# First batch of a pooled-attention and feed-forward kernel: V product and key transposes ahead of the scores, a second query buffer, weights touched two steps later

## The chip, the core and the metric

The kernel runs on one core of a Trainium2 chip. A core has five engines with a queue each: TensorE (PE in the profile; its weight loads are PEld), VectorE (DVE), ScalarE (ACT), GpSimd (POOL) and SyncE (SP, which here issues nearly all transfers). The metric is device time in microseconds, the median of the runs; lower is better.

## What is computed

Four batches of attention with 8 heads, 1152 keys and a head size of 64. The queries are averaged in pairs, so there are 576 of them. The output of all heads of a batch is the input of a feed-forward block with layer norm and a residual.

```python
q_pool = q.reshape(B, H, S // 2, 2, D).mean(axis=3)         # B, H, S, D = 4, 8, 1152, 64
scores = scale * np.matmul(q_pool, k.transpose(0, 1, 3, 2))
attn = softmax(scores)                                       # max, exp, sum, divide
x = np.matmul(attn, v)            # heads side by side: (4, 576, 512)
xn = (x - mean) / sqrt(var + 1e-6) * g_ln
out = x + np.maximum(xn @ w_ch1, 0.0) @ w_ch2                # 512 -> 2048 -> 512
```

All tensors are float32. Most products are done as three float16 products of high and low halves (`hi`, `lo`).

## The kernel before

**Steps.** The 32 heads form 16 pairs, a pair has C = 9 score tiles of 128 queries by 1152 keys, so there are 144 steps, numbered i, with p = i // 9 the pair. `step(i)` issues the work of one step to all engines in an order written out by hand; each engine then takes its own instructions strictly in that order and waits where data is missing. The first batch is pairs 0 to 3, steps 0 to 35; `on_pe(i)` is true there.

**One step of the first batch.** The scores S(i+1) go to three PSUM banks, 0 to 2 or 3 to 5 by turns (`slot`). DVE takes the row maximum (`emit_max`, L337) and makes the bias nb (L338), ACT takes the exponential into `pe` (`emit_exp`, L343), PE transposes `pe` in nine pieces back into the banks of the scores (`emit_t`, L376, called T(i) here), and ACT copies the result out to `pt` in two halves (`emit_t_copy`, L382). Because S(i+2) uses the same banks as S(i), it waits for these copies. The V product of an earlier tile (`emit_pv`, L400, PV here) is float32, and its result is scaled by 1/sum in `evac_pv` (DVE L446 and L449, ACT L453). In the later batches ACT and DVE make the halves `hl` instead, and a DMA transposes them (L369).

**What else is in the first batch.** The keys and queries of the next pair are transposed on PE, one piece a step (`prep_k`, `prep_q`, lines 275 to 289), and split into halves by ACT (L264) and DVE (L265). The 16 MB of float32 weights come in 32 pieces m of 512 KB, piece m issued in step m on SP (`w_load`, L633). ACT reads a piece first (`w_bias`, L638), then DVE passes over it three times (`w_conv`, L106), PE forms column sums of it (`w_sums`, L665), and after eight pieces a bound is reduced (`w_reduce`, and `all_max` at L194 to L203). POOL then splits four pairs of pieces into halves (`w_splits`, L238 and L721). Steps 36 to 143 add the feed-forward products as units (L534, L565).

**Order.** Lists say in which step a thing is issued: `pre(i, ...)` at the start of step i, `at(i, ...)` at its end. `fill` holds the DVE passes over weights, dripped one by one between other work; `evacs` holds what `flush` issues in the next step; `reds` the parts of a bound. The query tile `qr` holds two pairs and has one buffer; the bank pair 6 and 7 (`bank()`) takes the transposes of keys and queries.

The functions that the change touches follow with the line numbers of the profile.

Of the kernel before, what the change touches and what calls it, by code (L numbers as in the profile page):

```python
# [24 lines left out]
def tile_pooled_attention_moe(  # L25
# [158 lines left out]
    def all_max(src, n, then):  # L184
# [4 lines left out]
        def place():  # L189
            return psum[:, 3 * (pv_slot[0] % 2) + 2, 258:386]  # L190
# [18 lines left out]
    reds = deque()  # L209
# [51 lines left out]
    def split_from(ps, s, hi, lo):  # L261

        return (
            lambda: nc.scalar.activation(out=hi, in_=ps, func=ACTF.Copy, scale=s),  # L264
            lambda: nc.vector.scalar_tensor_tensor(lo, ps, s, hi, op0=ALU.mult, op1=ALU.subtract),  # L265
        )

    def prep_k(p, u):
# [3 lines left out]
        if u < 2:  # L272
# [3 lines left out]
            return split_from(ps, s[:, 0:1], kt[:, 0, u, 0:512], kt[:, 1, u, 0:512])  # L276
# [3 lines left out]
        return split_from(x, s[0:64, 0:1], kt[0:64, 0, :, 512:640], kt[0:64, 1, :, 512:640])  # L280

    def prep_q(p, u):
# [10 lines left out]
        return split_from(ps[:, 0:384], s[:, 1:2], qt[:, 0, c], qt[:, 1, c])  # L293
# [17 lines left out]
    def emit_s(i):  # L311
# [330 lines left out]
    def w_conv(m):  # L642
# [15 lines left out]
        later(lambda: sums.append(lambda: w_sums(part, 2 * c + z, lo)))  # L658
# [75 lines left out]

    for p in range(1, NP):
# [4 lines left out]
        if p % 2 == 0:  # L740
            at(i0 - 1, load_q, p, (nc.sync,))
# [115 lines left out]
    def some_units(i):  # L857
        if preps:
            fn, p, u = preps.popleft()
            evacs.extend(fn(p, u))  # L860
        for _ in range(1 if i < NSTEP + 5 else 2):
# [3 lines left out]
    def a_piece(i):  # L865
        pieces.extend(ready.pop(i, ()))
        for u in range(2 if len(pieces) > 2 else 1):
# [6 lines left out]
    def step(i):  # L874
# [15 lines left out]
        while sums and i % 2 == 0:  # L890
            sums.popleft()()
        flush()
        if live:
# [19 lines left out]
    with tc.manual_schedule():  # L913
# [52 lines left out]
        i = 0  # L966
# [32 lines left out]
```

## Time and profile before

| what | value |
|---|---|
| device time, median of 3 runs | 969.31 us (957.99, 969.43, 969.31) |
| span of the profiled execution | 963.9 us |
| PE busy | 880.9 us, 91% |
| DVE, ACT, POOL busy | 627.4, 549.9, 346.4 us |
| step 0's row maximum starts | 21.53 us |
| step 36's row maximum starts | 255.74 us |
| bytes moved | 114.92 MB |

For the profiled execution no device time is given beside its span; the span lies 5.4 us under the median and 5.9 us over the lowest run. Times in the profile count from the start of the span. A matmul's end is modelled, so neighbouring matmuls can overlap by some tenths. The busy shares are means over stages that differ: the first batch, steps 36 to about 130 in which attention and feed-forward overlap, and a tail with the feed-forward alone.

### The profile page before, as it was taken

The page shows a single profiled execution, that of the slowest core. Times are in us where ns is not written, and L with a number is a line of the kernel's source. Part 1 is how long each engine was busy: PE and PEld are TensorE (multiplying, and loading weights), DVE is VectorE, ACT ScalarE, POOL GpSimd, SP SyncE. Part 2 cuts the span into 40 slices and gives each one's busy share as a digit, 9 for nine tenths or more (in the row PEclk, how much of TensorE's full clock was granted, in tenths as well). Part 3 has the DMA queues.
Part 4 walks back from the last instruction along what each step waited for, and adds up shares of the span by engine and source line. Part 5 has one row for each costly group of instructions (what it writes and reads, how often), then busy time and mean ns, then how long its engine had stood idle before and what let it go on. Part 6 is the DMA issues. An engine that isn't in the chain of part 4 may idle for free.

```text
span 963.9 us, 21832 instructions
## 1 busy us (share of the span) xinstructions
PE 880.9 (91%) x9286; PEld 628.5 (65%) x9286; DVE 627.4 (65%) x1160; ACT 549.9 (57%) x779; POOL 346.4 (36%) x315
## 2 busy tenths in 40 slices
PE   5897988999869899989698999999989999999998
PEld 4676766777747476666474757566765766767665
DVE  4576696767787577757875777678777777542221
ACT  3765465655476677667667677676676766411000
POOL 3002165243579352435543424344534241310000
PEclk7897797968889999999999999999999999999999
DMA  5325152150155988698959596969596886600000
GB/s 156 145 70 183 66 177 69 48 183 1 50 99 106 191 125 171 129 197 133 179 102 209 102 198 129 187 131 174 101 208 118 168 143 116 122 23 12 12 12 22
DMA packets 271665, 114.92 MB, mean 119 GB/s; under 512 B 254928, under 2 KB 254928, under 8 KB 271568
## 3 DMA queue, kind: packets, MB, share of 16 engines
q1 hardware_dynamic: 271216, 112.65, 56.2%
q8 instruction: 72, 1.18, 0.5%
q10 hardware_dynamic: 352, 0.88, 0.3%
q14 instruction: 25, 0.20, 0.1%
HBM read 45.09 MB, written 4.72 MB: 52 GB/s over the span
## 4 chain that ended last, share of the span: by engine, by line
PE 57%; DVE 20%; ACT 9%; DMA 7%; issue 3%; SPq 3%; POOL 0%; ACTq 0%; DVEq 0%; POOLq 0%
PE psum L534 14%; PE psum L565 14%; PE psum L324 8%; PE psum L400 7%; PE psum L411 7%; DVE mx L337 5%; DMA pt<-hl 4%; DVE hl L366 4%; ACT pt L382 3%; PE psum L376 3%; DMA stage<-in_moe_w_ch_dram 2%; DVE ht L548 2%; PE psum L289 2%; SPq L128 2%; DVE kt L265 1%
## 5 line engine op out<-in xcount | busy, mean ns | idle before, releaser
L337 DVE TENSOR_REDUCE mx<-psum 128x1 f32<-128x1152 f32 x144 | 194.4, 1350 | 76.6 <-PE psum L400 39.6
L343 ACT ACTIVATE pe<-psum,nb,sc 128x1152 f32<-128x1152 f32 x144 | 188.9, 1312 | 29.5 <-DVE nb L338 28.2
L565 PE MATMUL psum<-wsl,ht 128*128 128x512 f16 x864 | 199.0, 383 | 0.2 <-DVE ht L548 0.2
L324 PE MATMUL psum<-kt,qt 64*128 64x512 f16 (+3 forms) x1440 | 166.3, 342 | 28.2 <-ACT pt L382 17.0
L534 PEld LDWEIGHTS <-wsl 128*128 128x128 f16 x1920 | 172.8, 99 | 25.1 <-issue 3.0
L534 PE MATMUL psum<-xn,wsl 128*128 128x256 f16 x1536 | 181.2, 277 | 2.1 <-DVE xn L504 1.1
L324 PEld LDWEIGHTS <-qt 64*128 64x128 f16 (+1 forms) x1440 | 70.6, 99 | 114.4 <-issue 76.0
L565 PEld LDWEIGHTS <-ht 128*128 128x128 f16 x864 | 82.5, 99 | 92.2 <-issue 4.3
L357 ACT ACTIVATE hl<-pe 128x1152 f16<-128x1152 f32 x108 | 125.7, 1164 | 19.5 <-DMA pt<-hl 16.2
L453 ACT ACTIVATE xb<-psum,r 128x64 f32<-128x64 f32 x128 | 40.1, 313 | 150.6 <-DVE r L449 142.1
L411 PEld LDWEIGHTS <-pt 128*128 128x128 f16 (+1 forms) x3240 | 108.9, 101 | 22.6 <-issue 22.1
L411 PE MATMUL psum<-vt,pt 128*128 128x65 f16 (+1 forms) x3240 | 120.5, 195 | 0.0
L366 DVE SCALAR_TENSOR_TENSOR hl<-pe,hl 128x1152 f16<-128x1152 f32 x72 | 104.9, 1457 | 0.0
L238 POOL TENSOR_SCALAR pe<-pe 128x1152 f32<-128x1152 f32 x36 | 42.0, 1166 | 153.9 <-ACT hl L357 143.6
L548 DVE SCALAR_TENSOR_TENSOR ht<-psum,ht 128x512 f16<-128x512 f32 x72 | 49.6, 690 | 72.6 <-ACT ht L547 71.8
L547 ACT ACTIVATE ht<-psum 128x512 f16<-128x512 f32 x72 | 42.8, 594 | 93.7 <-PE psum L534 93.3
L400 PE MATMUL psum<-vt,pt 128*128 128x65 f32 (+1 forms) x720 | 96.1, 298 | 0.0
L400 PEld LDWEIGHTS psum<-vt,pt 128*128 128x128 f32 (+1 forms) x720 | 91.9, 213 | 3.6 <-issue 3.4
L364 POOL TENSOR_TENSOR hl<-pe,hl 128x1152 f16<-128x1152 f32 x36 | 85.4, 2373 | 3.0
L382 ACT COPY pt<-psum 128x512 f32<-128x512 f32 x72 | 44.7, 639 | 55.9 <-PE psum L376 55.1
L161 POOL TENSOR_TENSOR qr<-qr 128x1152 f32<-128x1152 f32 (+1 forms) x8 | 22.3, 2786 | 130.2 <-DMA qr<-in_q_dram 94.6
L376 PE MATMUL psum<-ident,pe 128*128 128x128 f32 x324 | 51.7, 315 | 5.1 <-ACT pe L343 4.9
(104 smaller groups left out, 898.6 us busy)
## 6 DMA issues: line engine op xcount, KB each, us to landing
stage<-in_moe_w_ch_dram SPq DMA_DIRECT2D x32, 512.0 KB, 6.7
kr<-in_k_dram SPq DMA_DIRECT2D x16, 576.0 KB, 4.4
qr<-in_q_dram SPq DMA_DIRECT2D x31, 288.0 KB, 5.6
vr<-in_v_dram SPq DMA_DIRECT2D x15, 576.0 KB, 5.0
out_dram<-xb SPq DMA_DIRECT2D x32, 128.0 KB, 2.5
pt<-hl SPq DMA_TRANSPOSE x108, 4.8
vr<-in_v_dram ACTq DMA_DIRECT2D x1, 576.0 KB, 6.1
out_dram<-xh SPq DMA_DIRECT2D x4, 128.0 KB, 3.5
```

Of the source, the lines that this page charges most:

```text
L324: nc.tensor.matmul(out=sp[o:o + w, c0:c0 + n], lhsT=qt[r:r + 64, qa, q0:q0 + w], rhs=kt[r:r + 64, ka, h, k0:k0 + n], start=(a == 0), stop= ...
L337: nc.vector.tensor_reduce(mx, st["s"], axis=AX.X, op=ALU.max)
L343: nc.scalar.activation(out=st["pe"], in_=st["s"], func=ACTF.Exp, scale=pair[i // C]["sc"][:, 0:1], bias=st["nb"],)
L357: nc.scalar.activation(out=hl[:, 0], in_=st["pe"], func=ACTF.Copy, scale=2.0 ** 15)
L364: nc.gpsimd.tensor_tensor(hl[:, 1], st["pe"], hl[:, 0], op=ALU.subtract)
L366: nc.vector.scalar_tensor_tensor(hl[:, 1], st["pe"], 2.0 ** 15, hl[:, 0], op0=ALU.mult, op1=ALU.subtract)
L376: nc.tensor.transpose(st["s"][:, n], st["pe"][:, n], ident)
L382: nc.scalar.copy(st["pt"][:, a:b], st["s"][:, a:b])
L400: nc.tensor.matmul(out=dst, lhsT=pt[:, 128 * u + q0:128 * u + q0 + w], rhs=vt[:, h, c], start=(u == 0), stop=(u == C - 1),)
L411: nc.tensor.matmul(out=dst[:, 0:n], lhsT=lhsT, rhs=rhs, start=(u == 0 and lhsT is hi and n == 65), stop=(u == C - 1 and lhsT is lo), skip_ ...
L534: nc.tensor.matmul(out=ps[:, o:o + n], lhsT=wsl[:, 8 * w + cc, wa, f * 128:f * 128 + 128], rhs=xn[:, xa * KD + cc, 0:n], start=(m == 0), s ...
L565: nc.tensor.matmul(out=ps, lhsT=hv[0][:, ha, f, t * 128:t * 128 + 128], rhs=wsl[:, 8 * w + 4 + f // 2, wa, (f % 2) * DM:(f % 2) * DM + DM] ...
```

## The change

In steps of the first batch, `a_piece` (one PV) and `a_prep` (one piece of keys or queries) are now issued ahead of `emit_s(i + 1)`; PV takes a bank of `bank()` and no longer a part of the banks of the scores. The exponential is issued ahead of the flush; all three DVE passes over a weight piece are issued ahead of what evacuates PV. A part of a bound goes to the banks of the current step's tile (`place`) and is evacuated at the start of the next step (`found`). The column sums of parts 0 and 1 run in even steps, of parts 2 and 3 in odd ones. `qr` has two buffers, and the query load moves from step i0 - 1 to i0 - 2. `w_bias` of piece m moves from step m + 1 to m + 3, `w_conv` from m + 3 to m + 4, the reduction by one or two steps, the transposes of the next pair's keys and queries by one. On POOL, a copy of step 0's scale stands ahead of the pooling of pair 1's queries. The dummy matmuls at the start go from 70 to 110. The lines that only keep track of what is done (`have`, `need`) issue nothing.

```diff
-            r = raw_p.tile([128, 2, C, 2, D], FP32, tag="qr", name="qr")
+            r = raw_p.tile([128, 2, C, 2, D], FP32, tag="qr", name="qr", bufs=2)
...
         def place():
-            return psum[:, 3 * (pv_slot[0] % 2) + 2, 258:386]
+            u = this[0] if on_pe(this[0]) else pv_slot[0]
+            return psum[:, 3 * (u % 2) + 2, 258:386]
...
+    def behind_scales():
+        nc.gpsimd.tensor_copy(state(1)["acc"][0:64, 1:2], state(0)["sc"][0:64, 0:1])
+        nc.gpsimd.memset(state(1)["acc"][0:64, 1:2], 0.0)
...
-            at(i0 - 1, load_q, p, (nc.sync,))
+            at(i0 - 2, load_q, p, (nc.sync,))
...
-            pre(0, lambda: nc.gpsimd.memset(state(1)["acc"][0:64, 1:2], 0.0))
+            pre(0, behind_scales)
...
-            pre(i0 + (4, 5, 6, 6, 7, 8)[n], lambda fn=fn, p=p, u=u: preps.append((fn, p, u)))
+            late = 1 if on_pe(i0) else 0
+            pre(i0 + (4, 5, 6, 6, 7, 8)[n] + late, lambda fn=fn, p=p, u=u: preps.append((fn, p, u)))
...
-        at(i0 + 1, w_bias, m)
-        pre(i0 + 3, w_conv, m)
+        at(i0 + 3, w_bias, m)
+        pre(i0 + 4, w_conv, m)
         if m % 8 == 7:
-            at(i0 + 3, w_reduce, m // 8)
+            at(i0 + (5 if m < 16 else 4), w_reduce, m // 8)
...
-                ps = emit_pv(n, bank() if u else None)
+                ps = emit_pv(n, bank() if u or on_pe(i) else None)
...
             steps.pop(i - 1)
+            while found:
+                found.popleft()()
+        if on_pe(i):
+            a_piece(i)
+            a_prep()
         if i + 1 < NSTEP:
             emit_s(i + 1)
...
-        while sums and i % 2 == 0:
-            sums.popleft()()
-        flush()
-        if live:
+        while sums and i % 2 == sums[0][0] // 2:
+            sums.popleft()[1]()
+        if on_pe(i):
             emit_exp(i)
-            if not on_pe(i):
+            while fill:
+                drip()
+            flush()
+        else:
+            flush()
+            if live:
+                emit_exp(i)
                 emit_hi(i)
...
-        if reds:
-            evacs.append(reds.popleft()())
-        a_piece(i)
-        some_units(i)
-        if live and on_pe(i):
+        if on_pe(i):
             emit_t(i)
+            if reds:
+                found.append(reds.popleft()())
+        else:
+            if reds:
+                evacs.append(reds.popleft()())
+            a_piece(i)
+            a_prep()
+            some_units(i)
...
-        for _ in range(70):
+        for _ in range(110):
```

PE in a step of the first batch in which a piece of keys is transposed, before: `kt<-` and `qt` rows are scores, `vt,pt` is PV, `ident,kr` the keys' transposes, `ident,pe` is T(i).

```order
302 L324 MATMUL psum<-kt,qt 128x128
303 L400 MATMUL psum<-vt,pt 128x65 x9
304 L278 MATMUL psum<-ident,kr 64x128 x2
305 L376 MATMUL psum<-ident,pe 128x128 x9
306 L324 LDWEIGHTS qt
307 L324 MATMUL psum<-kt,qt 128x512
```

The same place on PE after the change:

```order
384 L383 MATMUL psum<-ident,pe 128x128 x9
385 L407 MATMUL psum<-vt,pt 128x65 x9
386 L282 MATMUL psum<-ident,kr 64x128 x2
387 L331 LDWEIGHTS qt
388 L331 MATMUL psum<-kt,qt 128x512
```

PV and the keys' transposes have moved from between the scores and T to between T and the next scores.

SP, from the first weight piece on, before: `stage` is a weight piece, `kr`, `vr` and `qr` the raw keys, values and queries of a later pair.

```order
5 L633 DMA stage<-in_moe_w_ch_dram 128x1024
6 L116 DMA kr<-in_k_dram 128x2x576
7 L116 DMA vr<-in_v_dram 128x2x576
8 L633 DMA stage<-in_moe_w_ch_dram 128x1024 x8
9 L116 DMA kr<-in_k_dram 128x2x576
10 L128 DMA qr<-in_q_dram 64x1152 x4
11 L633 DMA stage<-in_moe_w_ch_dram 128x1024
12 L116 DMA vr<-in_v_dram 128x2x576
```

The same place on SP after the change:

```order
5 L640 DMA stage<-in_moe_w_ch_dram 128x1024
6 L116 DMA kr<-in_k_dram 128x2x576
7 L116 DMA vr<-in_v_dram 128x2x576
8 L640 DMA stage<-in_moe_w_ch_dram 128x1024 x7
9 L128 DMA qr<-in_q_dram 64x1152 x4
10 L640 DMA stage<-in_moe_w_ch_dram 128x1024
11 L116 DMA kr<-in_k_dram 128x2x576
12 L640 DMA stage<-in_moe_w_ch_dram 128x1024
13 L116 DMA vr<-in_v_dram 128x2x576
```

The four query loads have moved ahead of a weight piece and of the keys.

DVE over one step, before: `mx` and `nb` are the row maximum and the bias, `r` the scaling of PV, the three L106 rows the passes over a weight piece.

```order
69 L337 TENSOR_REDUCE mx<-psum 128x1
70 L338 TENSOR_SCALAR nb<-mx,sc 128x1
71 L446 TENSOR_SCALAR r<-psum 64x2
72 L449 RECIPROCAL r<-r 64x2
73 L106 TENSOR_SCALAR stage<-stage 128x512
74 L106 SCALAR_TENSOR_TENSOR stage<-wsl,stage 128x512
75 L106 SCALAR_TENSOR_TENSOR wsl<-stage 128x512
76 L265 SCALAR_TENSOR_TENSOR qt<-psum,s,qt 128x384
```

The same place on DVE after the change:

```order
60 L344 TENSOR_REDUCE mx<-psum 128x1
61 L345 TENSOR_SCALAR nb<-mx,sc 128x1
62 L106 TENSOR_SCALAR stage<-stage 128x512
63 L106 SCALAR_TENSOR_TENSOR stage<-wsl,stage 128x512
64 L106 SCALAR_TENSOR_TENSOR wsl<-stage 128x512
65 L453 TENSOR_SCALAR r<-psum 64x2
66 L456 RECIPROCAL r<-r 64x2
67 L265 SCALAR_TENSOR_TENSOR qt<-psum,s,qt 128x384
```

The scaling of PV has moved behind the three passes; before, it belonged to the PV of the step before, now to the one of the same step.

## Rows read from the trace of the kernel before

**Rows 1.** Page: busy time by engine, and the granted clock in 40 slices (tenths)

```profile
PE 880.9 (91%) x9286; PEld 628.5 (65%) x9286; DVE 627.4 (65%) x1160; ACT 549.9 (57%) x779; POOL 346.4 (36%) x315
...
PEclk7897797968889999999999999999999999999999
```

**Rows 2.** Windows: length, busy time and count per engine, clock, DMA share, GB/s

```profile
39.06:71.85 32.79, 30.34 (x279) 24.40 (x277) 25.60 (x56) 22.22 (x36) 0.00 (x0) 1.00 0.17 52
71.85:114.30 42.45, 36.97 (x227) 29.61 (x228) 23.65 (x48) 19.45 (x31) 5.17 (x5) 0.68 0.37 115
114.30:144.12 29.82, 26.34 (x248) 21.11 (x247) 28.75 (x46) 18.72 (x31) 20.02 (x13) 1.00 0.51 177
195.38:227.41 32.03, 30.05 (x175) 24.25 (x174) 18.73 (x39) 17.44 (x28) 10.20 (x7) 0.63 0.44 139
39.06:255.74 216.68, 192.80 (x1504) 155.76 (x1502) 155.52 (x301) 121.79 (x195) 74.60 (x53) 0.84 0.27 89
300.00:963.90 663.90, 627.11 (x7247) 427.28 (x7243) 420.88 (x764) 379.46 (x516) 229.99 (x211) 0.98 0.67 127
```

**Rows 3.** Timeline, PE, one step at full clock: start, duration, instruction, idle before

```profile
46.36 0.97 PE L324 MATMUL psum<-kt,qt 64*128 64x512 f16 x8 [0.28 <-ACT pt L382]
47.26 2.22 PE L400 MATMUL psum<-vt,pt 128*128 128x65 f32 x18
...
49.54 1.19 PE L376 MATMUL psum<-ident,pe 128*128 128x128 f32 x9
50.85 0.37 PE L324 MATMUL psum<-kt,qt 64*128 64x512 f16 x1
```

**Rows 4.** Page and timeline, DVE: row maxima in all, of steps 0, 4, 10, 36

```profile
L337 DVE TENSOR_REDUCE mx<-psum 128x1 f32<-128x1152 f32 x144 | 194.4, 1350 | 76.6 <-PE psum L400 39.6
...
21.53 1.35 DVE L337 TENSOR_REDUCE mx<-psum 128x1 f32<-128x1152 f32 x1
...
39.06 1.36 DVE L337 TENSOR_REDUCE mx<-psum 128x1 f32<-128x1152 f32 x1 [4.23 <-PE psum L400]
...
71.85 1.36 DVE L337 TENSOR_REDUCE mx<-psum 128x1 f32<-128x1152 f32 x1 [1.02 <-PE psum L400]
...
255.74 1.36 DVE L337 TENSOR_REDUCE mx<-psum 128x1 f32<-128x1152 f32 x1 [0.52 <-PE psum L400]
```

**Rows 5.** Timelines of SP, ACT and PE around two waits for weights

```profile
72.40 2.39 SPq L128 DMA_DIRECT2D qr<-in_q_dram  x4
74.91 0.51 SPq L633 DMA_DIRECT2D stage<-in_moe_w_ch_dram  x1
...
81.69 0.66 ACT L638 ACTIVATE wsl<-stage 128x512 f32<-128x512 f32 x1 [4.46 <-DMA stage<-in_moe_w_ch_dram]
...
82.87 0.37 PE L324 MATMUL psum<-kt,qt 64*128 64x512 f16 x1 [4.15 <-ACT pt L382]
...
85.32 3.94 PE L400 MATMUL psum<-vt,pt 128*128 128x65 f32 x18
...
204.75 0.68 ACT L638 ACTIVATE wsl<-stage 128x512 f32<-128x512 f32 x1 [1.80 <-DMA stage<-in_moe_w_ch_dram]
```

**Rows 6.** Timeline: a DVE pass over weights alone, and one beside POOL

```profile
92.74 0.69 DVE L106 SCALAR_TENSOR_TENSOR wsl<-stage 128x512 int32<-128x512 int32 x1
...
124.80 2.13 POOL L721 TENSOR_TENSOR wsl<-wsl 128x1024 f16<-128x1024 f32 x1
124.83 2.65 DVE L106 SCALAR_TENSOR_TENSOR wsl<-stage 128x512 int32<-128x512 int32 x1
```

**Rows 7.** Timeline: the dummy matmuls, and the scales of pair 0

```profile
1.71 5.54 PE L932 MATMUL psum<-ident 128*128 128x128 f16 x70 [1.71 <-POOL ident L929]
...
10.42 0.27 PE L194 MATMUL psum<-ident,acc 128*3 128x128 f32 x1 [3.18 <-DVE acc L945]
...
12.31 2.61 POOL L161 TENSOR_TENSOR qr<-qr 64x1152 f32<-64x1152 f32 x1 [2.40 <-DMA qr<-in_q_dram]
...
12.47 2.48 DVE L231 TENSOR_SCALAR s<-s 128x3 f32<-128x3 f32 x1
```

**Rows 8.** Waits of PE from 300 us on (total, times, longest), and one of ACT

```profile
PE psum L194 <- ACT kt L179: 15.1, 5, 3.6
...
325.15 1.16 ACT L357 ACTIVATE hl<-pe 128x1152 f16<-128x1152 f32 x1 [3.84 <-DMA pt<-hl]
```

More of the change, by code (lines that the diff above doesn't have):

```diff
@@ L206, in all_max @@
         return one, two
-    reds = deque()
+    reds, found = deque(), deque()
     def scales_reduce(p, a=0, b=3, then=None):
@@ L259, in take_v, with split_from, low @@
         nc.gpsimd.tensor_tensor(vt[:, :, 66:66 + D], vr[:, h], vt[:, :, 0:D], op=ALU.subtract)
[L261 to L266, printed above, removed]
+    def split_from(what, ps, s, hi, lo):
+        def low():
+            nc.vector.scalar_tensor_tensor(lo, ps, s, hi, op0=ALU.mult, op1=ALU.subtract)
+            have.add(what)
+        return (lambda: nc.scalar.activation(out=hi, in_=ps, func=ACTF.Copy, scale=s), low)
+    have = set()
     def prep_k(p, u):
@@ L275, in prep_k @@
                 nc.tensor.transpose(ps[:, 128 * m:128 * m + 128], x, ident)
-            return split_from(ps, s[:, 0:1], kt[:, 0, u, 0:512], kt[:, 1, u, 0:512])
+            return split_from((p, "k", u), ps, s[:, 0:1], kt[:, 0, u, 0:512], kt[:, 1, u, 0:512])
         for h in range(2):
@@ L279, in prep_k @@
         x = ps[0:64, 0:256].rearrange("p (h n) -> p h n", h=2)
-        return split_from(x, s[0:64, 0:1], kt[0:64, 0, :, 512:640], kt[0:64, 1, :, 512:640])
+        return split_from((p, "k", 2), x, s[0:64, 0:1], kt[0:64, 0, :, 512:640], kt[0:64, 1, :, 512:640])
     def prep_q(p, u):
@@ L292, in prep_q @@
         c = slice(384 * u, 384 * u + 384)
-        return split_from(ps[:, 0:384], s[:, 1:2], qt[:, 0, c], qt[:, 1, c])
+        return split_from((p, "q", u), ps[:, 0:384], s[:, 1:2], qt[:, 0, c], qt[:, 1, c])
     PREPS = ((prep_k, 0), (prep_k, 2), (prep_q, 0), (prep_q, 1), (prep_k, 1), (prep_q, 2))
@@ L319, in emit_s @@
             parts = [(h, h * C * 64 + 128 * (j if h == 0 else j - 5), 128, 0)]
+        for h, q0, w, o in parts:
+            need = {(p, "k", h), (p, "k", 2), (p, "q", q0 // 384), (p, "q", (q0 + w - 1) // 384)}
+            assert need <= have, (i, need - have)
         for a, (ka, qa) in enumerate(((0, 0), (1, 0), (0, 1))):
@@ L657, in w_conv @@
         )
-        later(lambda: sums.append(lambda: w_sums(part, 2 * c + z, lo)))
+        later(lambda: sums.append((part, lambda: w_sums(part, 2 * c + z, lo))))
     def w_sums(part, u, mag):
@@ L855, in tile_pooled_attention_moe, with a_prep @@
     pieces = deque()
-    def some_units(i):
+    def a_prep():
         if preps:
@@ L860, in some_units @@
             evacs.extend(fn(p, u))
+    def some_units(i):
         for _ in range(1 if i < NSTEP + 5 else 2):
@@ L866, in a_piece @@
         pieces.extend(ready.pop(i, ()))
-        for u in range(2 if len(pieces) > 2 else 1):
+        for u in range(2 if len(pieces) > 2 and not on_pe(i) else 1):
             if pieces:
                 n = pieces.popleft()
-                ps = emit_pv(n, bank() if u else None)
+                ps = emit_pv(n, bank() if u or on_pe(i) else None)
                 evacs.extend(evac_pv(n, ps))
@@ L889, in step @@
             pv_slot[0] += 1
-        while sums and i % 2 == 0:
-            sums.popleft()()
-        flush()
-        if live:
+        while sums and i % 2 == sums[0][0] // 2:
+            sums.popleft()[1]()
+        if on_pe(i):
             emit_exp(i)
-            if not on_pe(i):
+            while fill:
[5 more added lines that the diff above has]
+                emit_exp(i)
                 emit_hi(i)
```

## The prediction

> **What bounds the kernel now.** I read the page first: PE is busy 91% of the span, far ahead of the other engines, but the granted clock is low in the first quarter alone [rows 1]. So the span splits in two. From 300 us on PE is busy 627.11 of 663.90 us at a clock of 0.98 [rows 2], and almost nothing is to be had there but by taking work off PE. The first batch is another thing. Its steps 4 to 36 (32 of them) last from 39.06 to 255.74 us [rows 4], which is 216.68 us or 6.77 us a step, at a mean clock of 0.84 [rows 2]. Next I cut that stretch by stage. Steps 4 to 10 run undisturbed at full clock: 32.79 / 6 = 5.46 us a step, of which PE is busy 30.34 / 6 = 5.06 us. Steps 10 to 15 take 42.45 us, 8.5 us each, at a clock of 0.68, and steps 28 to 32 take 32.03 us, 8.0 us each, at 0.63 [rows 2]. These two stages are where the time lies.
>
> What made them slow is read from the timelines [rows 5]. SP issued the query loads at 72.40 us, as its wait for the last transposes of the old queries ended, and the next weight piece only at 74.91, behind them. ACT's first touch of that piece stood idle for 4.46 us until it landed. Behind that touch on ACT stood the copies of the transposed tile, and behind those the next scores, so PE sat idle 4.15 us until 82.87. Then its clock was halved: PV took 3.94 us where it takes 2.22 at full clock [rows 3, 5]. At 204.75 the same instruction of ACT waits again, 1.80 us after work of its own had filled the rest.
>
> Within an undisturbed step the chain runs T(i), ACT's copy, scores, PV, T(i+1): PE starts one matmul of the scores after the first copy (0.37 us) and then waits 0.28 us for the second [rows 3]. That is all the order costs at full clock, 0.40 us a step (5.46 less 5.06).
>
> **The change part by part.** *PV and the transposes ahead of the scores.* They need 2.2 us and more, the two copies about 1.3, so the copies are covered by work that PE has anyway, and the 0.40 us of idle goes. Nothing is added to PE. I take the new undisturbed step at PE's busy time, 5.06 us. Its bounds are 4.8 (busy times of neighbours overlap by up to 0.16 us in [rows 3], and there are two or three seams) and 5.46 (nothing gained, because something else is late next). What is late next is DVE: 25.60 / 6 = 4.27 us a step, and ACT with 22.22 / 6 = 3.70 [rows 2], so the cover is thin but there.
>
> *PV in another bank.* In all, DVE sat idle 39.6 us before row maxima until a PV was done [rows 4], though the maximum doesn't read it; the two shared a bank. The Trainium skill, PSUM — Partial Sum Buffer, section PSUM bank collisions raise a hardware error, says that access should be guarded by bank, not by address; these waits agree with it. DVE was not the bound in these steps, so I count no gain of its own; it is the slack that DVE needs for a shorter step.
>
> *Weights touched two steps later, two query buffers.* The touch of a piece now comes three steps behind its issue, some 15 us, against one to two steps; the late piece landed 6.8 us after its issue (74.91 to 81.69) [rows 5]. And the query loads no longer wait for the old queries, so SP isn't held ahead of that piece. SP now waits for the old keys one DMA later, but only until PE's transposes early in the next step. I take both waits as gone, and with them the halved clock behind them. If a weight piece had to wait for its buffer the cover would be gone; the staging buffers are used again after 7 pieces, and the last reader of piece m now runs in step m + 5 or m + 6, so one step is left.
>
> *POOL beside DVE.* This doesn't go. A two-input pass of DVE takes 0.69 us alone and 2.65 beside POOL's 2.13 us subtraction [rows 6]. Steps 15 to 20 show the price at full clock: DVE busy 28.75 of 29.82 us for 5 steps while POOL worked 20.02 us [rows 2]. So these steps come down to DVE's 5.75 us, 0.69 over the undisturbed step, 3.45 us for 20.02 us of POOL. POOL works 74.60 us in the 32 steps, 3.73 times as much: 12.9 us. Bounds: 0 (the overlap hits spare time of DVE) and 3.73 x (29.82 - 5 x 5.06) = 16.9.
>
> *The 32 steps together:* 32 x 5.06 + 12.9 = 174.8 us against 216.68: **-41.9 us**. With the bounds: 32 x 5.46 + 16.9 = 191.6, -25; and 32 x 4.8 = 153.6, -63.
>
> *Other low clock.* The lost clock of the whole stretch is 0.16 x 216.68 = 34.7 us; the two stages of late weights hold 0.32 x 42.45 + 0.37 x 32.03 = 25.4 of it [rows 2]. The other 9.2 us came from short idle stretches of PE that had other causes. The sum above takes them as gone; I put half back: **+4.6** (0 to 9.2).
>
> *The start.* POOL's addition of 2.61 us held DVE's pass over three columns for 2.48 us, and all scales wait for that [rows 7]. The new copy on POOL reads the scale, so the addition comes behind it: -2.3, since a pass of that size should need a tenth or two. The 40 more dummy matmuls fill part of the 3.18 us that PE sits idle before the first bound; at 5.54 / 70 = 0.08 us each they would end at 1.71 + 110 x 0.08 = 10.4, as that bound's data come at 10.42 [rows 7], so they delay little. A clock that stays up until the first scores may give another 1 us (0 to 2). **-3.3** (-2.3 to -4.5). Steps 0 to 4 (21.53 to 39.06 [rows 4]) have no PV to move for the first three; I count nothing.
>
> *Later batches.* Only the query loads change. From 300 us on PE waited five times, 15.1 us in all, for a bound that ACT forms from values, keys and queries of the next pair [rows 8]. At the one of these that I followed, ACT stood behind an earlier instruction of its own that waited 3.84 us for a transposing DMA [rows 8], issued behind the query loads. A load one step earlier, with no wait in SP's queue, thins that crowd but leaves keys and values in it. I take a third, **-5** (0 to -15.1).
>
> *Sum:* -41.9 + 4.6 - 3.3 - 5 = -45.6, so the profiled span of 963.9 comes to 918.3. The runs' median lies 5.4 us over that span, and I carry this over: **924 us**.
>
> **The rivals.** *DVE sets the pace.* All three passes over a weight piece now stand in one block ahead of the scaling of PV, and a shorter step leaves POOL's work covering a larger share of the steps. For it: DVE's busy share of 28.75 in 29.82 us. Against: 4.27 us of DVE work in an undisturbed step. If every step ran like steps 15 to 20, 29.82 / 5 = 5.96 us: 32 x 5.96 = 190.7, -26.0, with the start -29.3, so 963.9 - 29.3 + 5.4 = 940 us. If in addition every two-input pass that meets POOL waited 1.96 us longer (2.65 less 0.69), two a step, a step beside POOL would take 4.27 + 3.9 = 8.2 us; 74.60 / 5.96 = 12.5 such steps and 19.5 of 5.06 give 201 us, -15.6, with the start -18.9: 950 us. The Trainium skill, SBUF — State Buffer, section Who interferes with whom, states that whichever of the two engines issues first holds the shared ports for its whole instruction and the other fully blocks, which would be this second figure. Rows 6 agree with it for one pass, but steps 15 to 20 came to 5.75 us of DVE and not 8.2, so few passes meet it in full.
>
> *The weights are still late.* If it is the crowd of transfers that makes the pieces late, and not their place behind the queries on SP, both stages stay as they are (74.5 us for 9 steps), and the other 23 steps gain 0.40 us: -9.2, with the start -12.5, so 957 us, no change that can be told. Against: the touch gains two whole steps.
>
> *The later half gains more.* If all five waits go, and with them the clock lost behind them, another 10 to 12 us: 913 us.
>
> *Slower.* PV in a bank of its own must wait until the bank is empty, and what empties it (r on DVE, then ACT) now stands behind three weight passes. If through that wait the scores lose their lead, all becomes one ring: maximum and bias 1.6, passes 1.8, scaling and its copy 0.6, PV 2.2, transposes 0.5, scores 1.0, in all 7.7 us a step: 32 x 7.7 = 246, +29.7 with -3.3 at the start: 996 us. It decides from 7.4 us a step on (+20 us). Against it: there are two banks and only 6 of 9 steps use the second for transposes; the scores of the next step are issued before the maximum that could hold them, and the ring then spans two steps.
>
> **How the numbers follow.** Chances: the forecast 0.65, DVE 0.15 (940 to 950), late weights 0.07, the later half 0.10, slower 0.03. The range leaves out slower and late weights, and reaches down to -67 (undisturbed steps of 4.9 us, which make -47, no low clock left, -4.5 at the start, -15.1 later) and up to the second figure of DVE's rival: 902 to 948 us. About 2% is what a measurement of this kernel can tell from no change: 949.9 and 988.7 us are the bounds. Faster: all of the forecast and of the later half, and most of DVE's, 0.88; within 2%: 0.09; slower 0.03.
>
> **What would show it.** In the profile of the changed kernel the row maxima of steps 4 and 36 should lie about 179 us apart (216.68 before) and step 0's should start near 18.2 us; ACT's first touch of weights should wait for no DMA; the clock should read near full from 40 to 215 us; the copies should end no wait of PE before the scores, and PE's idle time before T should wait for the exponential. DVE's share should exceed 0.9 while POOL splits weights. I am wrong if the clock still falls between steps 10 and 15, if PE waits for PV's bank, or if steps without POOL take over 5.5 us.

## The result, and the profile after the change

The changed kernel takes 924.37 us (median of 4 runs, 916.9 to 926.61) against 963.65 us before (4 runs on the same chip, 956.1 to 969.43): the ratio is 0.9584, with a 95% interval of 0.9509 to 0.9659. The profiled execution took 922.41 us with a span of 920.6, 43.3 us less than before; the forecast's sum was 45.6. The total is right, but two of its terms are not. By medians the gain is 39.3 us, since the kernel before came out at 963.65 us here and not at the 969.31 that the forecast started from.

The page after, against [rows 1]: PE's share, and where the granted clock still falls.

```profile
PE 860.8 (94%) x9326; PEld 617.4 (67%) x9326; DVE 625.1 (68%) x1160; ACT 547.3 (59%) x779; POOL 343.9 (37%) x316
...
PEclk8899889887589999999799999999999999999999
```

The windows after, cut at the same row maxima as [rows 2]: steps 4 to 10, 10 to 15, 15 to 20, 20 to 28, 28 to 32, 32 to 36, all 32, and the rest from 274 us on.

```profile
34.87:67.11 32.24, 30.25 (x295) 25.59 (x295) 25.33 (x54) 22.60 (x38) 3.77 (x2) 1.00 0.38 98
67.11:93.50 26.39, 23.93 (x229) 19.97 (x229) 20.54 (x48) 19.39 (x32) 1.52 (x3) 1.00 0.46 162
93.50:126.77 33.27, 29.02 (x237) 23.48 (x237) 27.49 (x48) 18.74 (x31) 16.73 (x12) 0.79 0.28 94
126.77:175.93 49.16, 42.58 (x393) 35.49 (x392) 41.59 (x79) 29.80 (x51) 25.00 (x17) 0.93 0.41 126
175.93:198.52 22.59, 19.31 (x159) 15.74 (x159) 16.84 (x40) 15.29 (x25) 2.15 (x3) 0.85 0.29 109
198.52:229.72 31.20, 24.74 (x211) 20.43 (x210) 25.07 (x41) 16.05 (x28) 19.11 (x16) 0.84 0.00 1
34.87:229.72 194.85, 169.82 (x1512) 140.71 (x1512) 156.86 (x303) 121.88 (x200) 68.28 (x52) 0.90 0.31 99
274.00:920.60 646.60, 624.15 (x7287) 426.27 (x7284) 422.82 (x767) 381.46 (x520) 234.87 (x214) 0.99 0.69 130
```

Beside the forecast, with 5.06 us a step and the price of POOL (12.9 us for 74.60 us of its work) spread by POOL's time in each stage of before:

| steps | before, us | forecast | after |
|---|---|---|---|
| 4 to 10 | 32.79 | 30.4 | 32.24 |
| 10 to 15 | 42.45 | 26.2 | 26.39 |
| 15 to 20 | 29.82 | 28.8 | 33.27 |
| 20 to 28 | 51.26 | 43.8 | 49.16 |
| 28 to 32 | 32.03 | 22.0 | 22.59 |
| 32 to 36 | 28.33 | 23.7 | 31.20 |
| all 32 | 216.68 | 174.8 | 194.85 |

The two stages of late weights came out as forecast, to within 0.6 us (for the second, steps 28 to 32, the cause is another matter, see below). The stages in which POOL works are the ones that failed: two of them became slower than before.

Three lines of DVE in steps 4 to 36 after show a wait that was not there (count, busy time, mean, then the idle time in front and what ended it):

```profile
L344 DVE TENSOR_REDUCE mx<-psum 128x1 f32<-128x1152 f32 x32 | 43.1, 1345 | 0.7 <-PE psum L331 0.7
...
L265 DVE SCALAR_TENSOR_TENSOR kt<-psum,s,kt 128x512 f16<-128x512 f32 (+1 forms) x11 | 7.2, 651 | 10.3 <-ACT kt L268 10.3
L265 DVE SCALAR_TENSOR_TENSOR qt<-psum,s,qt 128x384 f16<-128x384 f32 x11 | 6.8, 617 | 10.8 <-ACT qt L268 10.8
```

The wait of the row maxima for PV is gone (38.8 us in these steps before). But DVE's half of the split of keys and queries now waits 21.1 us for ACT's half, 0.96 us for each of 22 pieces; before it waited 1.0 in all:

```profile
L265 DVE SCALAR_TENSOR_TENSOR kt<-psum,s,kt 128x512 f16<-128x512 f32 (+1 forms) x11 | 7.1, 645 | 0.0
...
L265 DVE SCALAR_TENSOR_TENSOR qt<-psum,s,qt 128x384 f16<-128x384 f32 x11 | 6.7, 610 | 1.0 <-ACT qt L264 1.0
```

The timeline of one step beside POOL, the slow one from step 17 to 18, shows why:

```profile
106.33 1.35 DVE L344 TENSOR_REDUCE mx<-psum 128x1 f32<-128x1152 f32 x1
...
107.84 1.21 DVE L106 TENSOR_SCALAR stage<-stage 128x512 int32<-128x512 int32 x1
...
108.86 2.17 POOL L728 TENSOR_TENSOR wsl<-wsl 128x1024 f16<-128x1024 f32 x1
...
109.16 2.42 DVE L106 SCALAR_TENSOR_TENSOR stage<-wsl,stage 128x512 int32<-128x512 int32 x1
...
111.02 1.55 POOL L239 TENSOR_SCALAR wsl<-wsl,gs 128x1024 f32<-128x1024 f32 x1
111.61 1.49 DVE L106 SCALAR_TENSOR_TENSOR wsl<-stage 128x512 int32<-128x512 int32 x1
...
113.03 0.15 DVE L453 TENSOR_SCALAR r<-psum 128x1 f32<-128x1 f32 x1
...
113.46 0.31 ACT L460 ACTIVATE xb<-psum,r 128x64 f32<-128x64 f32 x1 [4.13 <-DVE r L456]
113.68 0.57 ACT L268 ACTIVATE qt<-psum,s 128x384 f16<-128x384 f32 x1
113.83 1.54 PE L407 MATMUL psum<-vt,pt 128*128 128x65 f32 x6 [1.22 <-ACT xb L460]
...
114.28 0.62 DVE L265 SCALAR_TENSOR_TENSOR qt<-psum,s,qt 128x384 f16<-128x384 f32 x1 [0.91 <-ACT qt L268]
...
114.82 1.35 DVE L344 TENSOR_REDUCE mx<-psum 128x1 f32<-128x1152 f32 x1
```

It is a ring. The three passes stretch to 5.1 us beside POOL; behind them on DVE stands r; ACT's `xb`, which needs r, stands idle for 4.13 us; behind `xb` on ACT stands the copy of the queries, and for that DVE waits ahead of its next maximum. PE's PV waits for `xb` too, because it needs the bank that `xb` empties. The step lasts 8.49 us; ten of the 32 steps last 7.0 us and more. Before the change fifteen did, eight of them in the two stages of late weights.

PE's waits over the whole span, against [rows 8]: the first two are new, the last was 15.1 in 5.

```profile
PE psum L407 <- ACT xb L460: 7.6, 6, 3.2
PE psum L407 <- ACT xh L460: 6.7, 3, 2.3
...
PE psum L331 <- ACT pt L389: 5.0, 13, 1.4
...
PE psum L195 <- ACT kt L179: 3.4, 3, 1.3
```

The third, the scores' wait for the copies, counted in steps 4 to 36 alone, before and after:

```profile
PE psum L324 <- ACT pt L382: 14.9, 34, 4.2
...
PE psum L331 <- ACT pt L389: 4.3, 11, 1.4
```

The start, against [rows 7]: the dummy matmuls end earlier than forecast (9.33 us), and DVE's pass over the scales no longer lasts 2.48 us.

```profile
1.70 7.63 PE L960 MATMUL psum<-ident 128*128 128x128 f16 x110 [1.70 <-POOL ident L957]
...
12.42 0.17 DVE L232 TENSOR_SCALAR s<-s 128x3 f32<-128x3 f32 x1
```

Row maxima, against [rows 4], are earlier by 2.6 us at step 0, 4.2 at step 4, 26.0 at step 36, 22.9 at step 48 and 43.3 from step 122 on. So steps 36 to 48 gave back 3.1 us, and the later batches gained 20.4, in five jumps, one for each query load of a later pair. Behind them lies one wait of ACT. Before the change, over the whole span:

```profile
ACT hl L357 <- DMA pt<-hl: 16.2, 5, 4.2
```

After it:

```profile
ACT hl L364 <- DMA pt<-hl: 3.8, 4, 1.9
```

SP's waits and its timeline before the change show what made that transposing DMA late: the query loads stood ahead of it on SP, and for those SP waited 19.0 us in 7 waits, until PE had transposed the old queries.

```profile
SPq L128 <- PE psum L289: 19.0, 7, 5.8
...
312.88 2.41 SPq L128 DMA_DIRECT2D qr<-in_q_dram  x4
315.41 6.23 SPq L369 DMA_TRANSPOSE pt<-hl  x1
321.69 0.58 SPq L116 DMA_DIRECT2D vr<-in_v_dram  x1
322.39 7.00 SPq L369 DMA_TRANSPOSE pt<-hl  x2
```

### The profile page after: what moved, and what is told of

Read it like the earlier page. It is cut to its first block, busy times and chain, and to the rows that moved or that the text cites. A ratio compares the mean times of both kernels' runs of the same rounds, so it can differ in the third digit from the quotient of the medians.

```text
span 920.6 us, 21982 instructions
## 1 busy us (share of the span) xinstructions
PE 860.8 (94%) x9326; PEld 617.4 (67%) x9326; DVE 625.1 (68%) x1160; ACT 547.3 (59%) x779; POOL 343.9 (37%) x316
## 4 chain that ended last, share of the span: by engine, by line
PE 49%; DVE 33%; ACT 9%; DMA 4%; issue 3%; POOL 1%; SPq 1%; ACTq 0%; DVEq 0%; POOLq 0%
PE psum L572 15%; PE psum L541 15%; DVE mx L344 8%; PE psum L418 6%; PE psum L331 6%; DVE stage L106 5%; DVE hl L373 4%; DVE wsl L106 3%; DVE kt L265 2%; ACT kt L268 2%; DVE ht L555 2%; PE psum L407 2%; ACT xb L460 2%; PE psum L293 1%; DVE nb L345 1%
## 5 line engine op out<-in xcount | busy, mean ns | idle before, releaser
L572 PE MATMUL psum<-wsl,ht 128*128 128x512 f16 x864 | 196.1, 380 | 0.2 <-DVE ht L555 0.2
L541 PEld LDWEIGHTS <-wsl 128*128 128x128 f16 x1920 | 170.8, 98 | 23.1 <-issue 2.9
L541 PE MATMUL psum<-xn,wsl 128*128 128x256 f16 x1536 | 177.4, 274 | 1.8 <-DVE xn L511 0.9
L331 PE MATMUL psum<-kt,qt 64*128 64x512 f16 (+3 forms) x1440 | 161.6, 348 | 10.5 <-ACT pt L389 5.0
L418 PEld LDWEIGHTS <-pt 128*128 128x128 f16 (+1 forms) x3240 | 108.0, 101 | 22.5 <-issue 22.1
L239 POOL TENSOR_SCALAR pe<-pe 128x1152 f32<-128x1152 f32 x36 | 41.9, 1164 | 176.1 <-ACT hl L364 165.8
L407 PE MATMUL psum<-vt,pt 128*128 128x65 f32 (+1 forms) x720 | 90.6, 288 | 14.4 <-ACT xb L460 7.6
L407 PEld LDWEIGHTS psum<-vt,pt 128*128 128x128 f32 (+1 forms) x720 | 86.6, 203 | 18.4 <-ACT xb L460 9.7
L265 DVE SCALAR_TENSOR_TENSOR qt<-psum,s,qt 128x384 f16<-128x384 f32 x48 | 29.6, 618 | 49.8 <-ACT qt L268 49.8
L265 DVE SCALAR_TENSOR_TENSOR kt<-psum,s,kt 128x512 f16<-128x512 f32 (+1 forms) x48 | 31.5, 659 | 46.9 <-ACT kt L268 46.9
L383 PE MATMUL psum<-ident,pe 128*128 128x128 f32 x324 | 48.6, 302 | 6.3 <-ACT pe L350 6.3
```

The lines of the kernel that those rows point to most:

```text
L331: nc.tensor.matmul(out=sp[o:o + w, c0:c0 + n], lhsT=qt[r:r + 64, qa, q0:q0 + w], rhs=kt[r:r + 64, ka, h, k0:k0 + n], start=(a == 0), stop= ...
L407: nc.tensor.matmul(out=dst, lhsT=pt[:, 128 * u + q0:128 * u + q0 + w], rhs=vt[:, h, c], start=(u == 0), stop=(u == C - 1),)
L418: nc.tensor.matmul(out=dst[:, 0:n], lhsT=lhsT, rhs=rhs, start=(u == 0 and lhsT is hi and n == 65), stop=(u == C - 1 and lhsT is lo), skip_ ...
L541: nc.tensor.matmul(out=ps[:, o:o + n], lhsT=wsl[:, 8 * w + cc, wa, f * 128:f * 128 + 128], rhs=xn[:, xa * KD + cc, 0:n], start=(m == 0), s ...
L572: nc.tensor.matmul(out=ps, lhsT=hv[0][:, ha, f, t * 128:t * 128 + 128], rhs=wsl[:, 8 * w + 4 + f // 2, wa, (f % 2) * DM:(f % 2) * DM + DM] ...
```

## The experiments

Kernels were run on three chips, each with the kernel before beside it, so kernels of different groups are compared by their ratio to it; an interval of a ratio reaches 0.005 to 0.009 to each side. Shifts of row maxima are against the profile of before. Each trace is of one execution, and executions differ: the kernel with late splits (below), whose first 30 steps are those of the changed kernel, is 3.8 us behind it at step 32. A shift of that size between two traces says little.

### The parts one by one

**Two query buffers alone**, in the kernel before:

```diff
-            r = raw_p.tile([128, 2, C, 2, D], FP32, tag="qr", name="qr")
+            r = raw_p.tile([128, 2, C, 2, D], FP32, tag="qr", name="qr", bufs=2)
...
-            at(i0 - 1, load_q, p, (nc.sync,))
+            at(i0 - 2, load_q, p, (nc.sync,))
```

> The kernel before with the second query buffer and the earlier query load alone. Theory: the gain behind step 44 (20 us in the changed kernel, in five jumps one per query load) comes from these two lines, so it is here as well, and the first wait for weights at step 11 shrinks, since that piece no longer stands behind loads that wait: 20 to 35 us under before, ratio 0.965 to 0.98. Rival: the jumps come from the new order or from a mere shift of the phases, then this kernel is within 5 us of before and has no jumps.

943.95 us, ratio 0.9711 (0.9626 to 0.9796). ACT no longer waits for a weight piece: steps 10 to 15 gain 14.6 us without any later touch. Its wait for transposing DMAs falls to 1.5 us, and the steps from 48 on gain 20.5 us. Both big gains of the change hang on this edit. The end is only 22.1 us earlier, because steps 4 to 10 lost 4.9 us and steps 15 to 28, with POOL beside them, 13.7; the clock was 0.86 in steps 15 to 20 and 0.72 in steps 20 to 28 there (1.00 and 0.90 before), and why was not settled.

**Weights touched later, alone**, in the kernel before:

```diff
-        at(i0 + 1, w_bias, m)
-        pre(i0 + 3, w_conv, m)
+        at(i0 + 3, w_bias, m)
+        pre(i0 + 4, w_conv, m)
...
-            at(i0 + 3, w_reduce, m // 8)
+            at(i0 + (5 if m < 16 else 4), w_reduce, m // 8)
```

> The kernel before with the weights touched two steps later alone. Theory: both waits for weights go (steps 10 to 15 and 28 to 32, 16 and 9 us in the changed kernel), nothing changes behind step 44: about 25 us under before, ratio 0.974. Rival: the order of PE is what took the waits off the path, then the two stages keep over half of their length above 5.5 us a step, 10 us under before at most.

952.7 us, ratio 0.9824 (0.9745 to 0.9903). The gain may be just under 1%. The trace is of an execution of 969.84 us, so only the waits are read from it. The touch waits for no DMA any more, but SP still waits 18.3 us in 7 for its query loads, and ACT now waits for the late queries themselves:

```profile
91.20 1.16 ACT L179 ACTIVATE qt<-qr 128x1152 f16<-128x1152 f32 x1 [2.09 <-POOL qr L161]
```

The later touch trades one late transfer for another; both stood behind SP's wait.

**Everything but the order**: before, with two query buffers, later weights and the new start.

```diff
+            r = raw_p.tile([128, 2, C, 2, D], FP32, tag="qr", name="qr", bufs=2)
...
+            pre(0, behind_scales)
...
+            at(i0 - 2, load_q, p, (nc.sync,))
...
+        at(i0 + 3, w_bias, m)
...
+        for _ in range(110):
```

> The kernel before with query buffers, later weights and the start, but with the old order of PV, transposes, bounds and DVE passes. Theory: the order gives nothing in sum, since it gains at most 2 us in steps without POOL work and loses as much beside it: within 5 us of the changed kernel, ratio 0.955 to 0.965 to before. Rival, the forecast's own term: the order is worth 32 x 0.40 = 13 us, so this one is 13 us slower than the changed kernel, ratio 0.972.

928.76 us, ratio 0.9583 (0.952 to 0.9645): the same as the changed kernel, which has 0.9584. So the order of PV and transposes, as written, is worth nothing that can be told. In the traces steps 4 to 36 last 201.78 us without it and 194.85 with it, and the end differs by 3.5 us. ACT's touch of weights waits for no DMA here, and still steps 28 to 32 last nearly as long as before the change (32.03 us), at a low clock:

```profile
181.71:211.26 29.55, 28.65 (x160) 23.03 (x157) 16.82 (x39) 16.03 (x25) 3.44 (x4) 0.57 0.20 72
```

**The changed kernel with one query buffer:**

```diff
-            r = raw_p.tile([128, 2, C, 2, D], FP32, tag="qr", name="qr", bufs=2)
+            r = raw_p.tile([128, 2, C, 2, D], FP32, tag="qr", name="qr")
...
-            at(i0 - 2, load_q, p, (nc.sync,))
+            at(i0 - 1, load_q, p, (nc.sync,))
```

> The changed kernel with one query buffer and the load at its old step. Theory: the five jumps behind step 44 go, 20 us more than the changed kernel, and the first batch stays within 3 us, since the touch of the weights is late enough without the buffer: ratio to before 0.978. Rival: the jumps stay, ratio 0.958; or the first batch falls back as well, ratio 0.99 and above.

942.85 us, ratio 0.9735 (0.9682 to 0.9788). SP waits 16.8 us in 7 again, ACT 12.7 us for transposing DMAs, and the steps from 48 on gain 7.3 us instead of 20.4. From the other side, this edit again carries most of the later gain. Why 7.3 us are left was not settled. The first batch did not stay within 3 us: steps 4 to 36 last 201.88 us (194.85 in the changed kernel), and steps 10 to 15 take 32.84 us at a clock of 0.79 (26.39 at 1.00), with ACT waiting 2.90 us for the late queries. So the later touch does not replace the buffer.

**The changed kernel with the old start:**

```diff
-            pre(0, behind_scales)
+            pre(0, lambda: nc.gpsimd.memset(state(1)["acc"][0:64, 1:2], 0.0))
...
-        for _ in range(110):
+        for _ in range(70):
```

> The changed kernel with 70 dummy matmuls and without the copy that holds POOL behind the scales. Theory, the forecast's start term: row maximum of step 0 about 2.5 us later, the whole 3 to 4 us slower than the changed kernel, ratio to before 0.962. Rival, from the two runs with the old start, whose clock stayed at half until 54 us: steps 0 to 8 also run at the low clock, 8 to 12 us slower, ratio 0.97.

925.89 us, ratio 0.9645 (0.958 to 0.971). In the traces row maximum 0 is 3.9 us later than in the changed kernel, step 4 is 6.0 and the end 4.4 us later. The ratios alone can't tell the start from nothing. But in all ten traces with the new start row maximum 0 starts at 17.66 to 19.44 us, in the four with the old one at 21.11 to 22.84: 3.4 us between the means.

### What slows the steps beside POOL

Theory one: POOL's work stretches DVE's passes, and DVE sets the pace. Theory two: the ring, with the scaling of PV behind the three passes. The next kernels take away one or the other.

**POOL's split passes left out** (in the changed kernel):

```diff
-        scaled(x, x, s)
+        scaled(x[:, 0:8], x[:, 0:8], s)
...
-        scaled(wsl[:, n, 0], x)
+        scaled(wsl[:, n, 0, 0:8], x[:, 0:8])
...
-        nc.gpsimd.tensor_tensor(wsl[:, n, 1], x, wsl[:, n, 0], op=ALU.subtract)
+        nc.gpsimd.memset(wsl[:, n], 0.03)
```

> The changed kernel in which POOL's three passes that split a pair of weight pieces work on 8 columns only and a constant is written instead (the feed-forward then has constant weights). Theory: DVE's passes beside POOL and the ring scaling of PV, its copy, PV's bank, scores, maximum make some 13 of the steps 12 to 36 last 7.6 us in place of 5.4, and those to 42 too; without the splits steps 15 to 36 come to 5.5 us, 136 to 115 us, and the kernel to 890 to 900 us, ratio 0.93. Rival, the forecast's price: 0.69 us a step beside POOL, 12.9 us in all, ratio 0.945. If DVE has spare time enough, nothing changes, 0.958.

908.82 us, ratio 0.9432 (0.9344 to 0.952), and steps 4 to 36 fall by 12.9 us, from 194.85 to 181.92: both as the rival said. POOL's other work stays:

```profile
35.24:217.16 181.92, 164.94 (x1517) 136.72 (x1517) 144.02 (x304) 122.20 (x200) 44.03 (x49) 0.93 0.33 106
```

DVE's passes are shorter (741 and 794 ns in place of 995), but its waits for ACT are what they were:

```profile
L265 DVE SCALAR_TENSOR_TENSOR kt<-psum,s,kt 128x512 f16<-128x512 f32 (+1 forms) x11 | 7.2, 651 | 10.3 <-ACT kt L268 10.3
L265 DVE SCALAR_TENSOR_TENSOR qt<-psum,s,qt 128x384 f16<-128x384 f32 x11 | 6.8, 618 | 10.8 <-ACT qt L268 10.8
```

So the 21.1 us are not the splits': they are there without them. The 12.9 us are.

**The scaling after two of the three passes** (in the changed kernel):

```diff
             emit_exp(i)
+            drip(2)
+            flush()
             while fill:
                 drip()
-            flush()
```

> The changed kernel with the scaling of PV on DVE ahead of the third pass over the weight piece instead of behind it. Theory: PE's waits for PV's bank (14.3 us in 9 waits) fall below 7 us, since beside POOL the third pass takes 1.4 to 2.6 us, and some low clock goes: 5 to 10 us less than the changed kernel, ratio 0.95. Rival: DVE itself sets these steps, and its sum doesn't change: within 3 us, the bank's waits turn into waits for the exponential.

904.69 us, ratio 0.9417 (0.9353 to 0.9481), more than the 5 to 10 us that I expected. Moving one call gives as much as leaving out all splits; against the kernel without the order (0.9583) the order with this call moved is worth 1.7%. The DVE lines in steps 4 to 36 here:

```profile
L265 DVE SCALAR_TENSOR_TENSOR kt<-psum,s,kt 128x512 f16<-128x512 f32 (+1 forms) x11 | 7.1, 648 | 2.5 <-ACT kt L268 2.3
L265 DVE SCALAR_TENSOR_TENSOR qt<-psum,s,qt 128x384 f16<-128x384 f32 x11 | 6.8, 614 | 2.3 <-ACT qt L268 2.3
```

4.8 us of idle in place of 21.1, with passes as long as before; PV's wait for its bank is 4.5 us in 5. The windows of steps 15 to 20 and of all 32:

```profile
89.03:118.19 29.16, 24.73 (x248) 20.52 (x246) 27.75 (x48) 18.77 (x31) 17.61 (x12) 1.00 0.39 132
...
35.22:208.37 173.15, 157.15 (x1515) 131.27 (x1516) 157.26 (x304) 123.57 (x200) 68.92 (x49) 0.97 0.35 111
```

DVE is busy for the same 157 us as in the changed kernel, in 21.7 us less, and in steps 15 to 20 for 95% of the time at full clock. The forecast's 174.8 us for the 32 steps is met here, in all stages to within 1 us but for steps 10 to 15 (23.22, forecast 26.2); steps 4 to 10 take 30.59 / 6 = 5.10 us each. So both theories hold a part of the changed kernel's cost: over the 32 steps the ring is the larger (21.7 us against 12.9), in steps 15 to 20 the splits are (29.16 us with the scaling early, 27.51 without splits, 33.27 in the changed kernel). With the scaling early, theory one describes what remains. No kernel has both edits, so whether the two parts add up was not tried.

**The splits of parts 2 and 3 ten steps later** (in the changed kernel):

```diff
-            i0 = this[0] + 1 + 3 * n // 2
+            i0 = this[0] + 1 + 3 * n // 2 + (10 if part > 1 else 0)
```

> The changed kernel with the splits of weight parts 2 and 3 ten steps later, when no pass over weight pieces is left on DVE. Theory: steps 32 to 42 lose POOL's company (7.5 us a step now) and come near 5.5 us, 15 us less by step 42; the splits then lie beside steps that PE sets, where they cost little: 8 to 15 us less than the changed kernel, ratio 0.945 to 0.95. Rival: the price moves along, to the passes that make the low halves, and the kernel stays within 3 us.

913.96 us, ratio 0.9515 (0.9447 to 0.9583). The gain lies in steps 32 to 42, as the theory said: 57.78 us, where the changed kernel takes 71.56. That step 42 is only 10 us earlier comes from the 3.8 us by which this execution was behind at step 32. Here, and then in the changed kernel:

```profile
202.32:260.10 57.78, 51.99 (x440) 39.94 (x442) 45.49 (x96) 38.89 (x58) 26.92 (x33) 0.79 0.30 67
...
198.52:270.08 71.56, 61.04 (x452) 47.30 (x450) 52.93 (x96) 39.30 (x58) 47.20 (x46) 0.71 0.27 58
```

**Both together:**

```diff
-            i0 = this[0] + 1 + 3 * n // 2
+            i0 = this[0] + 1 + 3 * n // 2 + (10 if part > 1 else 0)
...
+            drip(2)
+            flush()
             while fill:
                 drip()
-            flush()
```

> The scaling of PV behind two of the three weight passes (904.7 us by itself, the maximum of step 36 21 us earlier than in the changed kernel) and the splits of the feed-forward weights' later parts ten steps later (914.0 us, 8 us better at the end). Theory that both act on the same steps, those in which POOL works beside DVE and the scaling of PV comes late: once the scaling is early, moving POOL's work gives little more, the time is 900 to 905 us and step 36 lies no more than 3 us ahead of the kernel with early scaling. Rival, that the two are separate costs which add up: 893 to 897 us, step 36 about 8 us ahead.

893.99 us, ratio 0.9251 (0.9188 to 0.9314). The gains add up, as the rival said. The theory's own test, step 36, came out its way (2.9 us earlier than with early scaling alone), but it was the wrong place to look: steps 36 to 42 fall from 38.21 to 32.50 us. PE's clock was low there; the windows of these steps, with early scaling alone:

```profile
208.37:246.58 38.21, 32.51 (x239) 24.61 (x236) 27.48 (x56) 22.72 (x30) 27.78 (x32) 0.69 0.46 102
```

And with both:

```profile
205.44:237.94 32.50, 25.25 (x237) 19.14 (x235) 25.38 (x57) 22.53 (x30) 18.19 (x26) 0.84 0.54 118
```

**One pass ahead of the scaling, with late splits:**

```diff
-            drip(2)
+            drip(1)
```

> As the kernel with two passes ahead of the scaling and late splits, but with one pass ahead. If the only thing that counts is how early PV's bank is emptied, earlier is better still: 3 to 8 us faster than with two passes. If PV isn't ready by then, DVE stands idle in front of the scaling (0.4 to 0.7 us a step in undisturbed steps, of which DVE has 1.1 to spare), and the time is the same as with two passes or up to 10 us slower; the trace then shows DVE's reciprocal or the scaling's wait for PE with more idle time in front of it.

892.36 us, ratio 0.9217 (0.9158 to 0.9277): the same as with two. The waits for ACT's copies fall to 0.8 us, but r now waits 7.1 us for PV. This is the lowest time of the study.

**The scaling first, ahead of all three passes** (in the changed kernel, splits unmoved):

```diff
             emit_exp(i)
+            flush()
             while fill:
                 drip()
-            flush()
```

> The scaling of PV ahead of all three weight passes, the splits where the changed kernel has them. Against the kernel with two passes ahead (904.7 us): the reciprocal waits for PV's end, some 1.4 us of DVE idle a step, so an undisturbed step needs 4.3 + 1.4 = 5.7 us of DVE against PE's 5.1 to 5.4: 10 to 20 us slower than with two passes, 915 to 925 us. If the long ring through PV's bank is nearly all of the cost, the time stays within 5 us of 904.7.

911.1 us, ratio 0.9418 (0.9344 to 0.9492), as with two passes ahead (0.9417). The 10 to 20 us that I expected were not there. DVE's waits for ACT's copies are gone, and PV never waits for its bank; r waits 8.6 us for PV, and PE's T waits 13.5 us for the exponential (6.3 in the changed kernel). In the traces steps 4 to 36 last 179.19 us against 173.15, which the ratios don't bear out. What they show is that the scaling must not be last; how far ahead it stands makes no difference that can be told.

**One of POOL's passes on ACT** (two passes ahead, late splits):

```diff
-        scaled(wsl[:, n, 0], x)
+        nc.scalar.copy(wsl[:, n, 0].rearrange("p n -> p n"), x)
```

> As the kernel with two passes ahead and late splits, with one of POOL's passes over each feed-forward weight (the copy that rounds the upper half) on ACT. If POOL beside DVE is what is left of the cost, DVE's passes beside POOL become shorter and steps 15 to 40 gain 3 to 6 us. If ACT's exponentials and copies are held by the new passes (each stands ahead of the copy of the exponentials that the transposes wait for), the same steps lose 3 to 8 us.

898.16 us, ratio 0.9295 (0.9227 to 0.9363), no different from 0.9251. Both expectations came true, in different stages: steps 15 to 20 last 25.67 us (29.14 without the edit), steps 20 to 32 last 71.34 (65.15).

## Why the prediction was right, and where it wasn't

Span for span: steps 4 to 36 with their low clock gained 21.8 us where 37.3 were forecast, the start 4.2 for 3.3, everything behind step 36 17.3 for 5. The first error is 15.5 us too much, the others 12.3 and 0.9 too little; they cancel to 2.3. That they cancel is luck. So is part of the rest: the median lies 3.8 us over the profiled span and not the 5.4 that was carried over, which brings the error of the total below 1 us.

- *Late weights.* Right in cause and size for steps 10 to 15: 26.39 us where 26.2 were forecast, at a clock of 1.00. Which edit did it was left open; the query buffer alone does it (27.89 us at 1.00), the later touch alone doesn't free ACT. For steps 28 to 32 the size came out (22.59 us, forecast 22.0), but not for the reason given. I took the wait of 1.80 us that ends at 204.75 for what halved the clock there, but the clock was low before that wait began at 202.95, and PE was busy throughout it; window of before:

```profile
199.50:204.70 5.20, 5.20 (x25) 5.18 (x26) 3.00 (x6) 3.13 (x5) 1.04 (x1) 0.50 0.99 264
```

  And the kernel with everything but the order, which has no such wait, takes 29.55 us there at 0.57. What lowered the clock in that stage stays open.
- *PV and the transposes ahead of the scores.* The 32 steps are the term that was mis-sized: forecast -41.9, measured -21.8. PE's waits for the copies fell from 14.9 to 4.3 us in these steps (the forecast had them gone), and undisturbed steps shortened, but only to 5.37 us (steps 4 to 10, with 3.77 us of POOL in them), not 5.06. The step that failed is "steps 15 to 20 come down to DVE's 5.75 us": it took DVE as busy without a break. I had seen that the scaling now stands behind three passes, and made it the rival *Slower*, priced at 7.7 us a step in all 32, with a chance of 0.03. What I missed is what stands behind `xb` on ACT: the copies of keys and queries, which DVE needs ahead of its next maximum. So the ring closed through DVE, not only through PV's bank: some 1 us of idle DVE for each piece of keys or queries, with splits beside it or not, on top of the long passes. Ten steps ran at 7.0 to 8.55 us. With the scaling ahead of the last pass the 32 steps take 173.15 us, the forecast's size.
- *PV in another bank.* The wait of maxima for PV went as forecast. The sign that I gave for being wrong, PE waiting for PV's bank, came true: 14.3 us in 9 waits.
- *POOL beside DVE.* The price of a pass was right (995 ns mean, 1013 and 952 before), and so was the sum: leaving out the splits gives 12.9 us. The rival *DVE sets the pace* is not alone in holding the changed kernel (83% busy in steps 15 to 20, not over 90%); it is what holds the kernel with early scaling (95%). The range was to reach up to that rival's second figure, which is 950, and ends at 948; nothing hangs on it.
- *Other low clock.* 4.6 us were allowed for; the lost clock of steps 4 to 36 is 0.10 x 194.85 = 19.5 us. Most of it was lost in the stages beside POOL (0.79, 0.93 and 0.84), in which PE also waited for PV's bank; which idle time cost how much clock was not separated.
- *The start.* Right, a little too small.
- *Later batches.* Forecast -5, measured -20.4 from step 48 on. The row was there (ACT waiting 3.84 us for a transposing DMA), and I saw that it was issued behind the query loads. The step that failed is "thins that crowd but leaves keys and values in it": it was no crowd but SP's own queue, in which the query loads waited for their buffer and the transposing DMAs stood behind them. I also priced PE's wait of 15.1 us and took a third of it; with the clock that fell behind each wait (0.76 to 0.90 in the five places, 1.00 after) the whole was worth more; the clock's part was not measured apart.
- *The signs.* The row maxima of steps 4 and 36 lie 194.85 us apart (179 was named), and step 0's starts at 18.96 us (18.2). ACT's first touch waits for no DMA, and the clock stays up between steps 10 and 15, but not up to 215 us. DVE's share beside POOL is 0.83 and not over 0.9.

## What to carry to other kernels

When a load has one buffer and shares an in-order queue, list everything behind it in that queue, in every stage, before pricing a second buffer: here it was worth more than the reordering that the change was about, as that was written. When work is moved on an engine that runs in order, follow what is now behind it one engine further than the first waiter: don't put a scaling that frees a bank behind all other work of the step. Whether none, one or two of the three passes stood ahead of it made no difference that could be told. And a total that comes out right isn't proof of its terms: compare stage by stage, and look whether the clock fell before or behind the wait that you blame.

## What the runs showed of the hardware

**DVE beside POOL.** A two-input pass of DVE that meets a POOL pass isn't slowed in proportion: it ends a fixed time after the POOL instruction that it met at its start. In the timeline above, POOL's subtraction ends at 111.03 and DVE's pass at 111.58, 0.55 later; the next POOL pass ends at 112.57 and DVE's at 113.10, 0.53 later. Of the 64 such passes in the changed kernel, 22 overlapped an instruction of POOL. The 21 that began while it ran ended 0.52 to 0.56 us after its end; the one that began first took 0.69 us, as long as alone. The Trainium skill, SBUF — State Buffer, section Who interferes with whom, says that a pass of DVE with two inputs in SBUF contends with POOL's reads, and of the shared ports that whichever issues first holds them for its whole instruction while the other is fully blocked, not throttled; these rows agree with it. So the price of a meeting is what is left of the POOL instruction.

**TensorE's clock.** The kernel with two query buffers alone ran from 38 to 54 us at the lower of the two levels, with PE busy for 15.76 of 16.00 us (window of its trace: length, busy time of PE, PEld, DVE, ACT, POOL, clock):

```profile
38.00:54.00 16.00, 15.76 (x75) 13.42 (x72) 6.20 (x17) 4.16 (x8) 0.00 (x0) 0.51 0.00 1
```

So the clock stayed low for 16 us under a busy PE, and steps 4 to 10 of that execution took 4.9 us more than before. Why the clock came back when it did was not tried.
